# Later weight splits in the first expert, and another order of a word conversion's steps

## The chip, the core and the metric

One NeuronCore of a Trainium2 chip runs the whole program. The metric is the device time of one execution in microseconds. Five engines run side by side, each with its own queue in program order: TensorE (PE in the rows, its weight loads PEld), VectorE (DVE), ScalarE (ACT), GpSimd (POOL) and SyncE (SP, which here only issues DMAs).

## What is computed

Linear attention over 3072 tokens, then a mixture of eight experts where each token goes to one, then a small gated network. Cut to its lines:

```python
state = alpha[t] * state + k[t] v[t]          # per batch and head
y[t]  = q[t] @ state
# mixture: e = argmax(x @ w_gate)
out[e] = gate * sigmoid(x @ w_output_gate) * (relu(x @ w1[e]) @ w2[e])
# gated network; its weights arrive as 64-bit floats
out = ((x @ m1) * (x @ m2) @ m3) @ m_out
```

The gated network's weights are 64-bit floats, and the kernel makes 32-bit floats of them on the chip.

## The kernel before

**Stages.** Attention runs to about 130 us. The experts follow, ordered by size, with room for 464, 440, 424, 408, 396, 388, 376 and 360 tokens; I count them 0 to 7. Between experts 6 and 7 `w_prime` multiplies the last two matrices of the gated network (361 to 394 us). From 419 us on the gated network runs.

**Three-term products.** Each float is split into a high and a low part, and `mm3` (L154 to L157) issues three matmuls: high by high, high by low, low by high. `feed(n)` (L136 to L151) splits n more pieces of weights: ScalarE copies the raw piece to the high part (L146), VectorE subtracts it to get the low part (L147). When both pieces of a raw buffer are split, `load_ahead` has SP load the next raw buffer (L111, or L109 for weights that were converted on the chip). The split pieces live in two rings of four, one for an expert's up half and one for its down half.

**An expert.** The loop at its core has eight up steps (f = 0 to 7) and eight down steps. An up step (`e_up`) is nine matmuls into one of three PSUM banks of `ps_u`, then a ReLU on ScalarE (L822) and on VectorE the low part of it (L823), which frees the bank. A down step (`e_down`) is nine matmuls into three banks that stay. In down steps 1, 3 and 5 `x_split` turns and splits a third of the next expert's tokens (L772 ScalarE, L773 VectorE), and after step 5 GpSimd gathers the tokens of the expert after that (`x_gather`, L754). The order on every engine is the program's order (a manual schedule). So what `feed` puts on ScalarE in a step lies ahead of the ReLU of the next step.

**Steps of a side job.** In each up and down step the loop takes one `next(conv)` (two in expert 0's up half). In expert 0 `conv` is `late_routing`, small VectorE work that finds the tokens' places. From expert 1 on it is `convert_all`: it starts two loads, takes some empty steps, and then converts 23 buffers, each in four steps by `m_convert` (L855) and `words` (L116). A conversion reads pairs of 32-bit words from `mraw` (two buffers): ScalarE takes the absolute value of the high word into `cva` (two buffers, L121) and a scaled copy of the low word into `cvc` (one buffer, L122); VectorE does a maximum (L124), a shift (L125) and a combination with the sign (L127); GpSimd adds the two parts (L130) and writes the result back to memory (L856, `wm_d`). `read()` has SP load the buffer of two conversions later (L852).

Of the kernel before, what the change touches and what calls it, by code (L numbers as in the profile page):

```python
# [11 lines left out]
U32 = mybir.dt.uint32  # L12
ACTF = mybir.ActivationFunctionType
ALU = mybir.AluOpType
# [9 lines left out]
E = 8  # L24
# [28 lines left out]
def attention_then_moe_kernel(ctx, tc, pk0, pka, pkb, wbd_d, wexp, wmlp, cst_d, out):  # L53
    nc = tc.nc
    V, A, G, T, SP = nc.vector, nc.scalar, nc.gpsimd, nc.tensor, nc.sync
# [45 lines left out]
    def load_ahead(after=None):  # L101
        while loaded[0] < min(freed[0] + pools["keep"], len(units)):
            kind, i, parts = units[loaded[0]]
            raw = pools["raw"].tile([128, 2 * NPC], I32, tag="raw", name="raw")
            if after:
                after(raw[:, 0:1], 0)
            if kind == "r":
                for h in range(len(parts)):
                    SP.dma_start(out=raw.bitcast(F32)[:, h * NPC:(h + 1) * NPC], in_=wm_d[i + h])  # L109
            else:  # L110
                SP.dma_start(out=raw.bitcast(F32),  # L111
                             in_=wexp[bass.ds(first[i // 4] + i % 4, 1)].rearrange("o p n -> p (o n)"))
            raws[loaded[0]] = raw
            loaded[0] += 1

    def words(raw, read):  # L116
        w = raw.rearrange("p (n t) -> p n t", t=2)
        lw, hw = w[:, :, 0], w[:, :, 1]
        a, c = [pools["cv"].tile([128, NPC], I32, tag=t, name="cv" + t, bufs=n) for t, n in (("a", 2), ("c", 1))]
        af = a.bitcast(F32)  # L120
        A.activation(out=af, in_=hw.bitcast(F32), func=ACTF.Abs)  # L121
        A.activation(out=c, in_=lw.bitcast(U32), func=ACTF.Copy, scale=2.0 ** -29)  # L122
        yield
        V.tensor_scalar(out=af, in0=af, scalar1=TINY, scalar2=None, op0=ALU.max)  # L124
        V.tensor_scalar(out=a, in0=a, scalar1=3, scalar2=0x3FFFFFF8, op0=ALU.logical_shift_left, op1=ALU.bitwise_and)  # L125
        yield
        V.scalar_tensor_tensor(out=a, in0=hw, scalar=-(1 << 30), in1=a, op0=ALU.bitwise_and, op1=ALU.bitwise_or)  # L127
        read()
        yield
        G.tensor_tensor(out=a, in0=a, in1=c, op=ALU.add)  # L130
        return a.bitcast(F32)


    def ring(key):
        return {"e": key[-1] // 4, "o": 0, "3": 1, "m": key[-1] // 4}[key[0]]

    def feed(n):
        for _ in range(n):
            if fed[0] == len(stream):
                return  # L140
            u, c, key = stream[fed[0]]
            fed[0] += 1
            src = raws[u].bitcast(F32)[:, c * NPC:(c + 1) * NPC]
            tag = "w" + str(ring(key))
            hl = wring.tile([128, 2, NPC], F32R, tag=tag, name=tag)
            A.activation(out=hl[:, 0], in_=src, func=ACTF.Copy)  # L146
            V.tensor_tensor(out=hl[:, 1], in0=src, in1=hl[:, 0], op=ALU.subtract)  # L147
            pieces[key] = hl
            if c == len(units[u][2]) - 1:
                raws.pop(u)  # L150
                freed[0] += 1  # L151
                load_ahead()
# [329 lines left out]
    for j in range(NJ):  # L482
# [22 lines left out]
        if j == 5:  # L505
            A.activation(out=row, in_=cst[:, C_E4:C_E4 + E], func=ACTF.Copy, scale=1024.0)
            V.scalar_tensor_tensor(out=revc, in0=cst[:, C_E4:C_E4 + E], scalar=-1024.0 * E, in1=rev, op0=ALU.mult,
                                   op1=ALU.add)
# [7 lines left out]
        if j in R_RANK:  # L516
# [39 lines left out]
                           op0=ALU.mult, op1=ALU.add)  # L556
# [192 lines left out]
    def x_gather(e, after=None):  # L749
        xg[e] = xg_p.tile([128, 4, DM], F32, tag="xg", name="xg")  # L750
        if after is not None:
            A.activation(out=xg[e][:, :, 0], in_=after, func=ACTF.Copy)
        for i, n in tiles(width(e)):
            G.indirect_dma_start(  # L754
                out=xg[e][0:n, i, :], out_offset=None, in_=x_d[:, :],
                in_offset=bass.IndirectOffsetOnAxis(ap=idx_c[0:n, e, i:i + 1], axis=0))
# [58 lines left out]
    def e_up(e, f, w):  # L815
        m = width(e)
        ps = ps_u.tile([128, CMX], F32, tag="u", name="u")[:, 0:m]
        for k in range(KD):
            sl = slice((f % 2 * KD + k) * 128, (f % 2 * KD + k + 1) * 128)
            mm3(ps, w[:, 0, sl], w[:, 1, sl], xt[e][:, 0, k, 0:m], xt[e][:, 1, k, 0:m], k == 0, k == KD - 1)  # L820
        h = ht_p.tile([128, 2, CMX], F32R, tag=f"h{f}", name=f"h{f}")[:, :, 0:m]
        A.activation(out=h[:, 0, :], in_=ps, func=ACTF.Relu)  # L822
        V.scalar_tensor_tensor(out=h[:, 1, :], in0=ps, scalar=0.0, in1=h[:, 0, :], op0=ALU.max, op1=ALU.subtract)  # L823
        ht[f] = h

    def e_down(e, f, w, ds=range(KD)):
        for d in ds:
            if f == 0:
                dps[d] = ps_d.tile([128, CMX], F32, tag=f"d{d}", name=f"d{d}")[:, 0:width(e)]
            sl = slice(f % 2 * DM + d * 128, f % 2 * DM + d * 128 + 128)  # L830
            mm3(dps[d], w[:, 0, sl], w[:, 1, sl], ht[f][:, 0, :], ht[f][:, 1, :], f == 0, f == KF - 1)

    def e_store(e, col, ds=range(KD)):
        for d in ds:
            A.activation(out=yT[d][:, bass.ds(col, width(e))], in_=dps[d], func=ACTF.Copy)
# [3 lines left out]
    def y_split(g, ds=range(KD)):  # L839
        if ds[0] == 0:  # L840
            ys[g] = ys_p.tile([128, 2, KD, GRP], F32R, tag="ys", name="ys")
        for k in ds:
            src = yT[k][:, g * GRP:(g + 1) * GRP]
            A.activation(out=ys[g][:, 0, k], in_=src, func=ACTF.Copy)
            V.tensor_tensor(out=ys[g][:, 1, k], in0=src, in1=ys[g][:, 0, k], op=ALU.subtract)
# [3 lines left out]
    def m_load(i):  # L849
        if i < N_D:  # L850
            mraw[i] = pools["mr"].tile([128, 2 * NPC], I32, tag="mr", name="mraw")
            SP.dma_start(out=mraw[i], in_=wmlp_w[i])  # L852

    def m_convert(i):
        a = yield from words(mraw.pop(i), lambda: m_load(i + 2))  # L855
        G.dma_start(out=wm_d[i], in_=a)  # L856
        yield
# [94 lines left out]
    def convert_all():  # L952
        m_load(0)
        m_load(1)
        for _ in range(4):
            yield
        for i in range(N_D):
            yield from m_convert(i)

    for e in range(E):  # L960
        if e == 1:
            for _ in conv:
                pass
            lr.close()
            pools["cv"] = cv2.enter_context(tc.tile_pool(name="cvb", bufs=1, reuse_waits="tile"))
            pools["mr"] = cv2.enter_context(tc.tile_pool(name="mr", bufs=2, reuse_waits="tile"))
            conv = convert_all()
        for f in range(KF):
            e_up(e, f, pieces["e", e, f // 2])
            if f % 2:  # L970
                pieces.pop(("e", e, f // 2))
            if e == 0 or f % 2 or e == E - 1:
                feed(1)
            for _ in range(1 if e else 2):
                next(conv, None)
            if e == 0 and f == 1:
                x_gather(1, ht[1][:, 0, 0:4])
        if e == E - 1:
            for d in range(KD):
                for f in range(KF):  # L980
                    e_down(e, f, pieces["e", e, 4 + f // 2], [d])
                e_store(e, offs[e], [d])
                y_split(0, [d])
            for f in range(4):
                pieces.pop(("e", e, 4 + f))
            break
        for f in range(KF):
            e_down(e, f, pieces["e", e, 4 + f // 2])
            if f % 2:
                pieces.pop(("e", e, 4 + f // 2))  # L990
                feed(1)
            next(conv, None)
            if f in (1, 3, 5):
                x_split(e + 1, f // 2, xg[e + 1])
                if f == 5 and e + 2 < E:
                    x_gather(e + 2)
        e_store(e, offs[e])
        if e == E - 2:
            w_prime()
# [136 lines left out]
```

## Time and profile before

| what | us |
|---|---|
| median of 3 runs | 732.04 |
| lowest and highest of them | 731.51, 733.71 |
| the profiled execution, whole | 734.38 |
| its span, first to last instruction | 732.6 |
| TensorE matmul busy | 689.3 (94%) |
| VectorE busy | 400.3 (55%) |
| ScalarE busy | 338.0 (46%) |
| GpSimd busy | 208.4 (28%) |

The profile is of one execution. A row of a timeline gives the start, the duration, the engine, the line and what it writes and reads; in brackets stands how long the engine was idle before it and what ended that. A matmul's end is modelled, so the weight loads (PEld) show more plainly when TensorE really went on.

### The profile page before, as it was taken

To read this page: it belongs to the slowest core of one execution; us is meant where nothing else is said; L and a number is where in the kernel's file an instruction comes from. 1 tells how busy PE (TensorE), PEld (TensorE's weight loads), DVE (VectorE), ACT (ScalarE), POOL (GpSimd) and SP (SyncE) were. 2 spreads that over 40 slices of the span, in tenths; PEclk is the share of its full clock that TensorE was granted. 3 is DMA by queue.
4 is the path that set the end of the run, shared out by engine and by line. 5 is a ranking of instruction groups with operands and counts; after the bars stand their busy time and mean duration, and the time that the engine had idled before them with its cause. 6 is when DMAs were issued, how large, how long until landed. Compare 5 with 4: busy or idle time off the path is not lost.

```text
span 732.6 us, 14570 instructions
## 1 busy us (share of the span) xinstructions
PE 689.3 (94%) x5856; PEld 610.3 (83%) x5856; DVE 400.3 (55%) x723; ACT 338.0 (46%) x666; POOL 208.4 (28%) x233
## 2 busy tenths in 40 slices
PE   6989998789999999998999999999999999999993
PEld 3877787378999998997999988988889889889893
DVE  6989897678689778687734565033132231340320
ACT  3787786344656756656634554133122222331320
POOL 2977685225153544435310000200101101002001
PEclk7999999899999999999999999999999999999997
DMA  8899883464686887878644500100000000001000
GB/s 275 234 256 252 247 261 109 139 214 162 221 296 234 303 285 262 299 250 297 216 150 152 173 1 0 44 1 12 32 1 22 21 1 34 11 1 44 0 12 33
DMA packets 28200, 101.73 MB, mean 139 GB/s; under 512 B 4784, under 2 KB 5208, under 8 KB 28128
## 3 DMA queue, kind: packets, MB, share of 16 engines
q1 hardware_dynamic: 21360, 77.26, 32.9%
q0 software_dynamic: 6624, 23.29, 9.2%
q8 instruction: 47, 0.77, 0.4%
q14 instruction: 25, 0.20, 0.1%
q10 hardware_dynamic: 144, 0.20, 0.1%
HBM read 82.25 MB, written 18.48 MB: 138 GB/s over the span
## 4 chain that ended last, share of the span: by engine, by line
PE 64%; DVE 4%; issue 4%; POOL 3%; ACT 2%; DMA 2%; POOLq 0%; ACTq 0%
PE pab L157 9%; PE pab L155 9%; PE pab L156 9%; PE o L157 4%; PE o L156 4%; PE o L155 4%; PE d L155 4%; PE u L155 4%; PE d L156 4%; PE d L157 4%; PE u L157 4%; PE u L156 4%; POOL cva L130 3%; DVE w L147 2%; ACT w L146 1%
## 5 line engine op out<-in xcount | busy, mean ns | idle before, releaser
L147 DVE TENSOR_TENSOR w<-raw,w 128x768 fp32r<-128x768 f32 x87 | 103.5, 1193 | 57.6 <-ACT w L146 56.3
L1029 DVE TENSOR_TENSOR p_s<-pab,a_s 128x512 f32<-128x512 f32 x48 | 33.2, 692 | 168.4 <-PE pab L157 168.4
L1043 POOL DMA_INDIRECT out_dram<-o_s,idx_o x24 | 23.4, 974 | 331.6 <-ACT o_s L1042 327.9
L155 PE MATMUL pab<-ys,w 128*128 128x512 f32 x288 | 113.8, 395 | 0.0
L157 PE MATMUL pab<-ys,w 128*128 128x512 f32 x288 | 113.8, 395 | 0.0
L156 PE MATMUL pab<-ys,w 128*128 128x512 f32 x288 | 113.8, 395 | 0.0
L146 ACT ACTIVATE w<-raw 128x768 fp32r<-128x768 f32 x87 | 73.0, 842 | 51.6 <-PE d L157 21.2
L1031 ACT ACTIVATE ab<-p_s 128x512 fp32r<-128x512 f32 x48 | 30.4, 634 | 105.5 <-DVE p_s L1029 105.5
L155 PE MATMUL u<-xt,w 128*128 128x464 f32 (+7 forms) x192 | 69.0, 360 | 8.8 <-DVE h L823 8.1
L130 POOL TENSOR_TENSOR cva<-cva,cvc 128x768 int32<-128x768 int32 x23 | 47.0, 2044 | 95.9 <-ACT cva L121 32.4
L156 PE MATMUL u<-xt,w 128*128 128x464 f32 (+7 forms) x192 | 67.6, 352 | 1.5 <-DVE xt L773 1.5
L155 PE MATMUL d<-h,w 128*128 128x464 f32 (+7 forms) x192 | 68.9, 359 | 0.0
L157 PE MATMUL u<-xt,w 128*128 128x464 f32 (+7 forms) x192 | 67.2, 350 | 0.0
L156 PE MATMUL d<-h,w 128*128 128x464 f32 (+7 forms) x192 | 66.9, 348 | 0.0
L157 PE MATMUL d<-h,w 128*128 128x464 f32 (+7 forms) x192 | 66.6, 347 | 0.0
L157 PEld LDWEIGHTS pab<-ys,w 128*128 128x128 f32 x288 | 54.0, 187 | 13.3
L156 PEld LDWEIGHTS pab<-ys,w 128*128 128x128 f32 x288 | 54.0, 187 | 12.9
L155 PEld LDWEIGHTS pab<-ys,w 128*128 128x128 f32 x288 | 54.0, 187 | 12.9
L155 PE MATMUL o<-wpp,ab 128*128 128x384 f32 x192 | 64.2, 334 | 0.0
L157 PE MATMUL o<-wpp,ab 128*128 128x384 f32 x192 | 64.2, 334 | 0.0
L156 PE MATMUL o<-wpp,ab 128*128 128x384 f32 x192 | 64.2, 334 | 0.0
L1032 DVE TENSOR_TENSOR ab<-p_s,ab 128x512 fp32r<-128x512 f32 x48 | 33.2, 693 | 33.6 <-ACT ab L1031 33.6
(187 smaller groups left out, 1436.1 us busy)
## 6 DMA issues: line engine op xcount, KB each, us to landing
raw<-in_wexp_dram SPq DMA_DIRECT2D x32, 768.0 KB, 5.1
mraw<-in_wmlp_dram SPq DMA_DIRECT2D x23, 768.0 KB, 4.3
pb<-in_pkb_dram SPq DMA_DIRECT2D x24, 384.0 KB, 5.0
wm_d<-cva POOLq DMA_DIRECT2D x23, 384.0 KB, 3.9
raw<-wm_d SPq DMA_DIRECT2D x23, 384.0 KB, 3.7
pa<-in_pka_dram SPq DMA_DIRECT2D x42, 192.0 KB, 4.9
x_d<-xs POOLq DMA_DIRECT2D x23, 192.0 KB, 4.6
pa<-in_pka_dram SPq DMA_DIRECT2D x42, 97.5 KB, 5.1
```

The lines of the kernel that those rows point to most:

```text
L130: G.tensor_tensor(out=a, in0=a, in1=c, op=ALU.add)
L146: A.activation(out=hl[:, 0], in_=src, func=ACTF.Copy)
L147: V.tensor_tensor(out=hl[:, 1], in0=src, in1=hl[:, 0], op=ALU.subtract)
L155: T.matmul(out=ps, lhsT=sh, rhs=mh, start=start, stop=False)
L156: T.matmul(out=ps, lhsT=sh, rhs=ml, start=False, stop=False)
L157: T.matmul(out=ps, lhsT=sl, rhs=mh, start=False, stop=stop)
L1029: V.tensor_tensor(out=p_s, in0=pss[1], in1=a_s, op=ALU.mult)
L1031: A.activation(out=t[:, 0], in_=p_s, func=ACTF.Copy)
L1032: V.tensor_tensor(out=t[:, 1], in0=p_s, in1=t[:, 0], op=ALU.subtract)
L1043: G.indirect_dma_start(out=out[:, :], out_offset=bass.IndirectOffsetOnAxis(ap=idx_o[:, n:n + 1], axis=0), in_=o, in_offset=None)
```

## The change

Two places of the loop over experts, one number and the order of `words` are changed.

- In expert 0's up half `feed(1)` is called in steps 3 to 7 and no longer in all eight; in its down half it is called in steps 0 to 5 and 7 and no longer in the odd ones alone. Twelve calls before, twelve after.
- `convert_all` takes five empty steps, not four.
- A conversion's four steps before: both ScalarE passes; maximum and shift; the combination and the load; the addition and the write-back. After: the absolute value; all three VectorE passes; nothing; the copy of the low word, the load, the addition and the write-back.

```diff
         A.activation(out=af, in_=hw.bitcast(F32), func=ACTF.Abs)
-        A.activation(out=c, in_=lw.bitcast(U32), func=ACTF.Copy, scale=2.0 ** -29)
         yield
         V.tensor_scalar(out=af, in0=af, scalar1=TINY, scalar2=None, op0=ALU.max)
         V.tensor_scalar(out=a, in0=a, scalar1=3, scalar2=0x3FFFFFF8, op0=ALU.logical_shift_left, op1=ALU.bitwise_and)
-        yield
         V.scalar_tensor_tensor(out=a, in0=hw, scalar=-(1 << 30), in1=a, op0=ALU.bitwise_and, op1=ALU.bitwise_or)
+        yield
+        yield
+        A.activation(out=c, in_=lw.bitcast(U32), func=ACTF.Copy, scale=2.0 ** -29)
         read()
-        yield
         G.tensor_tensor(out=a, in0=a, in1=c, op=ALU.add)
         return a.bitcast(F32)
...
         m_load(0)
         m_load(1)
-        for _ in range(4):
+        for _ in range(5):
             yield
...
             if f % 2:
                 pieces.pop(("e", e, f // 2))
-            if e == 0 or f % 2 or e == E - 1:
+            if f > 2 if e == 0 else f % 2 or e == E - 1:
                 feed(1)
...
             if f % 2:
                 pieces.pop(("e", e, 4 + f // 2))
+            if f % 2 or e == 0 and f < 6:
                 feed(1)
             next(conv, None)
```

## Rows read from the trace of the kernel before

**Rows 1.** The page, part 2: granted TensorE clock in 40 equal slices, in tenths.
```profile
PEclk7999999899999999999999999999999999999997
```

**Rows 2.** Busy time by stretch (start:end, length, engines with counts, granted clock, DMA).
```profile
154.30:157.70 3.40, 3.40 (x10) 2.93 (x9) 2.87 (x8) 2.75 (x7) 1.82 (x2) 0.50 0.60 193
147.30:181.10 33.80, 31.49 (x161) 26.89 (x160) 28.16 (x70) 14.90 (x26) 14.23 (x14) 0.95 0.56 191
```

**Rows 3.** Waits of weight loads (us, times, longest): 143-181; 200-360, two; 394-420.
```profile
PEld u L155 <- DVE h L823: 2.7, 1, 2.7
...
PEld u L155 <- DVE h L823: 8.6, 11, 1.2
...
PEld u L156 <- DVE xt L773: 1.9, 2, 1.6
...
PEld u L155 <- DVE h L823: 1.4, 2, 0.9
```

**Rows 4.** Timelines of ScalarE and TensorE, expert 0 and the start of expert 1.
```profile
149.99 0.85 ACT L146 ACTIVATE w<-raw 128x768 fp32r<-128x768 f32 x1 [3.42 <-DMA raw<-in_wexp_dram]
...
153.74 0.48 PE L155 MATMUL u<-xt,w 128*128 128x464 f32 x1 [2.31 <-DVE h L823]
...
154.66 0.59 PE L155 MATMUL u<-xt,w 128*128 128x464 f32 x1
155.04 0.59 PE L156 MATMUL u<-xt,w 128*128 128x464 f32 x1
...
157.94 0.37 PE L155 MATMUL u<-xt,w 128*128 128x464 f32 x1
158.15 0.38 PE L156 MATMUL u<-xt,w 128*128 128x464 f32 x1
...
181.73 0.36 PE L155 MATMUL u<-xt,w 128*128 128x440 f32 x1
```

**Rows 5.** Groups by line, 200 to 360 us: busy, mean ns, idle before, releaser.
```profile
L121 ACT ACTIVATE cva<-mraw 128x768 f32<-128x768 f32 x21 | 19.2, 913 | 9.8 <-DMA wm_d<-cva 9.8
L122 ACT ACTIVATE cvc<-mraw 128x768 int32<-128x768 uint32 x21 | 19.1, 909 | 26.5 <-POOL cva L130 26.4
...
L147 DVE TENSOR_TENSOR w<-raw,w 128x768 fp32r<-128x768 f32 x43 | 60.1, 1397 | 21.3 <-ACT w L146 21.0
L127 DVE SCALAR_TENSOR_TENSOR cva<-mraw,cva 128x768 int32<-128x768 int32 x21 | 19.9, 947 | 0.0
L125 DVE TENSOR_SCALAR cva<-cva 128x768 int32<-128x768 int32 x21 | 12.4, 591 | 0.7
L124 DVE TENSOR_SCALAR cva<-cva 128x768 f32<-128x768 f32 x21 | 11.6, 553 | 0.0
...
L130 POOL TENSOR_TENSOR cva<-cva,cvc 128x768 int32<-128x768 int32 x21 | 42.8, 2036 | 75.1 <-ACT cva L121 32.4 <-issue 18.9 <-ACT xt L772 8.8
```

**Rows 6.** Timelines of expert 5's up half: ScalarE, VectorE, GpSimd, weight loads.
```profile
304.68 0.51 ACT L822 ACTIVATE h<-u 128x388 fp32r<-128x388 f32 x1
...
314.00 0.90 ACT L121 ACTIVATE cva<-mraw 128x768 f32<-128x768 f32 x1 [2.30 <-DMA wm_d<-cva]
...
309.42 0.96 DVE L147 TENSOR_TENSOR w<-raw,w 128x768 fp32r<-128x768 f32 x1 [0.17 <-ACT w L146]
...
313.17 2.42 DVE L147 TENSOR_TENSOR w<-raw,w 128x768 fp32r<-128x768 f32 x1
...
307.65 0.62 POOL L856 DMA_DIRECT2D wm_d<-cva  x1 [0.30 <-POOL cva L130]
312.93 1.84 POOL L130 TENSOR_TENSOR cva<-cva,cvc 128x768 int32<-128x768 int32 x1 [4.66 <-issue]
...
309.31 0.19 PEld L155 LDWEIGHTS u<-xt,w 128*128 128x128 f32 x1 [0.25 <-DVE h L823]
311.97 0.19 PEld L155 LDWEIGHTS u<-xt,w 128*128 128x128 f32 x1 [1.13 <-DVE h L823]
```

**Rows 7.** ScalarE's timeline, first up step of expert 7.
```profile
399.03 0.84 ACT L146 ACTIVATE w<-raw 128x768 fp32r<-128x768 f32 x1 [2.15 <-DMA raw<-in_wexp_dram]
```

More of the change, by code (lines that the diff above doesn't have):

```diff
@@ L125, in words @@
         V.tensor_scalar(out=a, in0=a, scalar1=3, scalar2=0x3FFFFFF8, op0=ALU.logical_shift_left, op1=ALU.bitwise_and)
+        V.scalar_tensor_tensor(out=a, in0=hw, scalar=-(1 << 30), in1=a, op0=ALU.bitwise_and, op1=ALU.bitwise_or)
         yield
-        V.scalar_tensor_tensor(out=a, in0=hw, scalar=-(1 << 30), in1=a, op0=ALU.bitwise_and, op1=ALU.bitwise_or)
+        yield
+        A.activation(out=c, in_=lw.bitcast(U32), func=ACTF.Copy, scale=2.0 ** -29)
         read()
-        yield
         G.tensor_tensor(out=a, in0=a, in1=c, op=ALU.add)
```

## The prediction

> **What bounds the kernel now.** I read the page first: TensorE is the bound and runs at the full granted clock nearly everywhere, so only its holes can be won [rows 1]. Then the waits of its weight loads, stretch by stretch, because a hole in the loads is a hole in the matmuls [rows 3]: in the first expert one wait of 2.7 us for the VectorE subtraction at L823 (it frees one of the three `ps_u` banks); from 200 to 360 us, experts 2 to 6 (numbered from 0), eleven such waits, 8.6 us, and two for VectorE's split of the next tokens, 1.9 us; in the last expert 1.4 us. After that the matmul phases have no holes. Both halves of the change aim at those 10.5 and 2.7 us.
>
> *First expert.* ScalarE stood 3.42 us until 149.99 for a raw weight that had not landed: the split that up step 0 puts into its queue [rows 4]. Behind it in the same queue lay the ReLU of step 1; TensorE, which had used up its three banks, waited for VectorE's half of it and started again at 153.74. Then the granted clock fell to half (0.50 from 154.3 to 157.7) [rows 2]: matmuls follow each other every 0.38 us there and every 0.21 us after [rows 4].
>
> *Experts 2 to 6.* Two queues are blocked by the word conversion. On ScalarE, the copy of the low word (L122) waits 26.4 us in 21 conversions for GpSimd's addition, because `cvc` has one buffer and its last reader runs only one step earlier; `Abs` (L121) waits 9.8 us for the write-back of two conversions before [rows 5]. ReLUs lie behind both. On VectorE, the split takes 2.42 us where GpSimd's addition started just before it (312.93 and 313.17), and ends 0.82 us behind that addition's end [rows 6]; the mean over the stretch is 1.40 where a free one takes 0.96 (309.42). Additions that start second are longer in turn, 2.04 in the mean against 1.84 for that one [rows 5, 6].
>
> **Part 1, later splits in the first expert.** Nothing is added or removed. The first split after the start moves from up step 0 to up step 3, those behind it likewise, until down step 5, where both orders stand level; each split's ScalarE copy and VectorE subtraction and the raw load that SP issues behind it move along. The weight of 149.99 is now asked for behind the ReLU of step 3 (about 151.4), when it has long landed. So the 2.7 us [rows 3] go, and with no such hole I expect no half clock: nine matmuls at 0.38 in place of 0.21 are 1.6 us. Sum 4.3. What is late next: VectorE, busy 28.2 of the 33.8 us behind the first ReLU [rows 2], with 4.3 us less to do it in. Its last item that TensorE needs is the third token split of the next expert; that stretch ends with it. Without any idle time it would end at 181.1 - 5.6 = 175.5; I leave 1.8 of idle time in front of raw loads, 177.3. TensorE began expert 1 at 181.73 [rows 4] and needs it six matmuls (1.2) later; 4.3 earlier that is 178.6. It fits by 1.3, so I charge 0.2 only. SP's raw loads of the next expert start up to 2 us later (my estimate from the same queue); a split that has to wait for one then waits in the down half, where no ReLU lies behind it. Value -4.1, bounds -4.4 and -2.1 (room overrun by 2).
>
> **Part 2, the conversion's order.** Work stays the same: two ScalarE passes (0.91 each), three VectorE passes (0.55, 0.59, 0.95), one addition (1.84 when free), one load on SP, one write-back on GpSimd's queue [rows 5, 6]. With the fifth empty step at the start, `Abs` falls on up and down steps 1 and 5, the three VectorE passes on 2 and 6, nothing on 3 and 7, the copy, the load and the addition on 4 and 0. Step by step:
>
> - The copy of L122 now follows the previous addition by four steps, over 6 us: its 26.4 us of waiting [rows 5] go. New wait: the addition now waits for this copy. Behind it on GpSimd lie only the write-back and, once per expert, the token gather, needed an expert later.
> - VectorE: before, `max`, shift and a split stood ahead of the ReLU half of step 2; now the three passes stand on steps without a split. The additions start at steps 0 and 4, behind the copy, where VectorE has only PSUM reads or nothing to do, except as below.
> - SP: the load of the word pairs leaves one to two steps later and behind the raw load of steps 3 and 7; the write-back likewise goes out later. `Abs` is one step later too, so room shrinks by a step. I measured one write-back from 307.65 to the `Abs` at 314.00 that it held, 6.3 us [rows 6]. In the new order up step 5 may still wait a microsecond for it, but behind step 5 no ReLU holds a bank that this expert's up half still needs. So I cost it nothing; if that cover fails it is part of the bounds.
>
> A walk through expert 5, the second narrowest of these: its first ReLU is at 304.68 [rows 6] in both orders. The copy behind it ends near 305.97, the addition runs from 306.1 to 307.94, the split of step 1 ends 0.82 later, 308.76; then ReLU half of step 2, three passes (0.55, 0.59, 0.95) and ReLU half of step 3, done near 311.6. Before, the same half of step 2 came so late that TensorE stood 1.13 us until 311.97, with a hole of 0.25 at 309.31 ahead of it [rows 6]. In the new order, step 2's half is done at 309.2 and TensorE asks for it at 310.3 (311.97 - 1.13 less that hole and the 0.3 that the shorter of the two token-split waits cost [rows 3]); step 3's is late by 0.0 to 0.1. So 10.5 us of holes less 0.3 for such edges.
>
> The narrow place: the split of step 3 starts near 311.5; the addition of step 4 starts behind ReLU 4 and the copy, near 312.1. Half a microsecond decides who is first; in expert 6, with shorter matmuls, about 0.25. If the addition is first, the split ends 0.82 behind it, some 2 us late, and the ReLU half of step 4 holds up step 7 by about 1.9. The Trainium skill's page SBUF — State Buffer, section "Who interferes with whom", says the same as a rule: the port pair that VectorE and GpSimd share goes to whoever starts first, for its whole instruction. The trace agrees, with 2.42 us for the split behind an addition and a mean of 2.04 for the additions [rows 5, 6]; by that rule the order of starts alone makes the sum 9.0 or 4.8. I take 1.2 off for it (the narrowest expert, a bit more than even). Value -9.0, bounds -10.5 (all holes) and -4.8 (collisions in experts 4 to 6, three times 1.9 kept).
>
> **Part 3, the spill into the last expert.** Four empty steps and 23 conversions of four made 96 steps, exactly experts 1 to 6. With five, the last copy (0.91), addition (1.84) and write-back fall into up step 0 of expert 7, where a split stands on every step. That split waits for its weight until 399.03 [rows 7]; the copy comes behind it and holds the next ReLU, which TensorE waited for (1.4 us in all, two holes [rows 3]). Then the addition blocks a split, 1.46 us by 2.42 against 0.96 [rows 6]. ScalarE's next wait for a weight swallows part. Value +0.7, bounds 0 and +1.4. The vacated steps in front of `w_prime` free nothing, TensorE has no hole there.
>
> **Sum.** -4.1 -9.0 +0.7 = -12.4. Against the profiled execution's own time, 734.38: 722.0. The median of the three runs, 732.04, is 2.34 lower: 719.6.
>
> **Rivals.**
> 1. *The collision moves to step 4.* The addition beats the split in experts 4 to 6. For it: margins of 0.25 to 0.5 us in a hand-made queue. Against: GpSimd's start follows three ScalarE instructions. 5.7 us stay: 734.38 -4.1 -4.8 +0.7, as a median 723.8.
> 2. *The conversion's waits only change their names.* The write-back or the pair load, asked for later, hold `Abs` at steps where ReLUs count. For it: 6.3 us for a write-back. Against: two whole conversions lie between. Only the first expert pays: -4.1 +0.7, 728.6.
> 3. *The first expert doesn't pay.* VectorE is the bound of its down half and hands the hole back: -9.0 +0.7, 723.7.
> 4. *Slower.* The collision at step 4 comes in all of experts 2 to 6 and its 1.9 us stop is long enough for the clock to halve, as after the 2.7 us stop [rows 2, 3]; stops of up to 1.6 us were not followed by that [rows 1, 3]. Then 1.9 + 1.6 = 3.5 in five experts is 17.5 for the 10.5 taken away: +7.0 -4.1 +0.7 = +3.6, 735.6. It decides once step 4's copy starts 0.8 us earlier against VectorE than I reckon, and only if 1.9 us of rest suffice.
>
> **How the numbers follow.** Forecast 0.68; rival 1 0.17; rival 2 0.06; rival 3 0.05; rival 4 0.04. The lowest sum is -4.4 -10.5 +0 = -14.9, 717.1, with run-to-run spread 716.5; the highest within the forecast and rivals 1 and 3 is -2.1 -4.8 +1.4 = -5.5, 726.5, say 727. That leaves rivals 2 and 4 and a little of the edges outside. A measurement of this kernel tells 0.3%, 2.2 us, from no change. All but rival 4 lie beyond it on the fast side, rival 2 by little, so some of it goes to "same": faster 0.92, same 0.04, slower 0.04.
>
> **What would show it.** Part 1: no ScalarE wait for a raw weight ahead of the second ReLU, no hole near 151, clock 1.00 through 160, and expert 1 starting about 4 us earlier. Part 2: L122 with no wait for GpSimd; L121's wait for the write-back much below 9.8 or only at steps 5; the split's mean between 1.0 and 1.2, with at most one blocked split per expert in its up half, behind step 0's addition; the eleven holes down to a handful of a tenth. Rival 1 would show as one hole of nearly 2 us ahead of up step 7. Part 3: a copy and an addition near the start of expert 7 and a slightly larger hole there. I am wrong if a wait for DMA takes ScalarE's time in up steps 0 to 4, or if the token split of the next expert becomes the late item.

## The result and the profile after

The changed kernel takes 726.65 us in the median of five runs (725.14 to 727.38), beside 732.04 (731.01 to 734.06) before: a ratio of 0.9912, interval 0.9891 to 0.9932. I had forecast 719.6 with a range of 716.5 to 727.0. So it is faster and within the range, but by 5.4 us where I had worked out 12.4, at the far end.

The page of the kernel after: its first lines, part 2's granted clock, and two lines of part 6 (size, median us from issue to landing).

```profile
PE 687.8 (95%) x5856; PEld 612.2 (84%) x5856; DVE 397.1 (55%) x723; ACT 338.9 (47%) x666; POOL 209.2 (29%) x233
...
PEclk9999999799999999998999999999999999999998
...
mraw<-in_wmlp_dram SPq DMA_DIRECT2D x23, 768.0 KB, 6.7
wm_d<-cva POOLq DMA_DIRECT2D x23, 384.0 KB, 5.6
```

Against [rows 1] the slice around 136 us reads 7 where it read 8, and there is a new 8 around 335 us. On the page of before the last two medians are 4.3 and 3.9 us: the same bytes now land later.

The waits of the weight loads after, for the stretches of [rows 3]: 200 to 352 us, then 384 to 412 (L155, L156). Between 143 and 181 us there is no row for `h` any more, only `issue` of 0.7 us in all.

```profile
PEld u L155 <- DVE h L823: 3.4, 2, 2.4
...
PEld u L155 <- DVE h L823: 2.0, 2, 1.2
PEld d L156 <- DVE h L823: 0.3, 1, 0.3
```

Of eleven holes two are left, 3.4 us, both behind 320 us, in expert 6. Groups by line after, 200 to 352 us, to be read against [rows 5]:

```profile
L128 ACT ACTIVATE cvc<-mraw 128x768 int32<-128x768 uint32 x21 | 19.1, 911 | 0.0
L121 ACT ACTIVATE cva<-mraw 128x768 f32<-128x768 f32 x21 | 19.0, 903 | 10.0 <-DMA wm_d<-cva 7.1 <-DMA mraw<-in_wmlp_dram 2.9
L147 DVE TENSOR_TENSOR w<-raw,w 128x768 fp32r<-128x768 f32 x42 | 52.2, 1249 | 18.0 <-ACT w L146 17.2
```

The copy's 26.4 us of waiting are gone. The split's mean fell from 1397 to 1249 ns. But `Abs` waits as long as before, 10.0 us, now for a load too.

To place the difference I took the length of each half of an expert (from its first weight load to the first of the next half). Columns are kernels, a number behind a name being another profiled execution of it; halves that are not listed are equal within 0.15 us in all.

```
              before before_2 after after_2 after_3 p1_feeds p2_words drain c_early  a3   a3_drain a3_drain_2 b_c2 b_small
start of e0   143.07 141.50  140.99 142.47 140.44  143.09   141.26  141.49 140.93 142.81  141.19   142.46  142.44 138.87
e0 up          19.75  19.38   17.02  17.06  15.61   17.38    19.33   16.92  17.09  15.61   18.05    18.14   19.38  19.47
e0 down        18.71  18.70   18.71  18.71  18.70   18.70    18.71   18.71  18.73  18.71   18.70    18.71   19.16  18.99
e2 up          14.12  14.12   13.88  13.88  13.88   14.11    13.88   13.88  13.88  13.88   13.88    13.88   14.12  13.88
e3 up          14.44  14.48   13.41  13.41  13.41   14.49    13.41   13.41  14.04  13.41   13.41    13.41   13.98  13.41
e4 up          14.88  14.89   12.96  12.96  12.96   15.22    12.96   12.96  13.74  12.96   12.96    12.96   13.83  12.96
e5 up          15.23  15.25   12.81  12.81  12.81   15.39    12.81   12.81  13.62  12.81   12.81    12.81   13.76  12.81
e6 up          16.49  16.44   18.16  14.80  16.46   17.41    15.82   14.86  15.58  14.13   12.52    12.37   14.86  13.72
e7 up          13.16  13.09   13.80  13.52  13.65   13.44    13.83   12.79  12.89  13.72   13.29    12.89   13.09   12.84
e7 down        11.92  11.91   12.18  11.96  11.99   11.90    12.01   11.85  11.97  11.98   11.85    11.91   11.91   11.92
```

The two profiled executions are 7.7 us apart: 2.1 because expert 0 starts earlier, 2.7 in expert 0, 5.6 in experts 2 to 5, less 1.8 lost in expert 6 (0.1 of it in its down half) and 0.9 in expert 7. The 2.1 are not the change's: nothing before expert 0 was touched, and the starts of one and the same kernel lie 1.6 to 2.0 us apart (143.07 and 141.50 before; 140.99, 142.47 and 140.44 after).

**Expert 5 came out as walked through.** Timelines of its up half after (start, duration, engine, line; in brackets the idle time before), to be read against [rows 6]:

```profile
296.66 0.51 ACT L822 ACTIVATE h<-u 128x388 fp32r<-128x388 f32 x1
297.03 0.93 ACT L128 ACTIVATE cvc<-mraw 128x768 int32<-128x768 uint32 x1
...
305.85 0.92 ACT L121 ACTIVATE cva<-mraw 128x768 f32<-128x768 f32 x1 [0.26 <-DMA wm_d<-cva]
...
299.23 1.49 DVE L147 TENSOR_TENSOR w<-raw,w 128x768 fp32r<-128x768 f32 x1 [0.17 <-ACT w L146]
303.63 0.95 DVE L147 TENSOR_TENSOR w<-raw,w 128x768 fp32r<-128x768 f32 x1
...
305.63 1.49 DVE L147 TENSOR_TENSOR w<-raw,w 128x768 fp32r<-128x768 f32 x1
...
298.05 1.86 POOL L130 TENSOR_TENSOR cva<-cva,cvc 128x768 int32<-128x768 int32 x1 [1.66 <-ACT cvc L128]
304.16 2.15 POOL L130 TENSOR_TENSOR cva<-cva,cvc 128x768 int32<-128x768 int32 x1 [3.34 <-ACT cvc L128]
```

The split of step 1 ends at 300.72, 0.81 us behind the addition's end at 299.91. The split of step 3 starts 0.53 us ahead of the second addition and takes 0.95 us; the addition pays instead, with 2.15. I had reckoned with half a microsecond. The split of step 5 then starts while that addition still runs (until 306.31), and takes 1.49 us: two splits of this half are blocked, and neither makes a hole.

**Expert 6 didn't.** Timelines after: ScalarE, weight loads, GpSimd, VectorE and SP.

```profile
314.06 0.90 ACT L121 ACTIVATE cva<-mraw 128x768 f32<-128x768 f32 x1 [2.44 <-DMA wm_d<-cva]
...
329.21 0.89 ACT L121 ACTIVATE cva<-mraw 128x768 f32<-128x768 f32 x1 [3.57 <-DMA wm_d<-cva]
329.99 0.85 ACT L822 ACTIVATE h<-u 128x376 fp32r<-128x376 f32 x2
...
331.11 0.19 PEld L155 LDWEIGHTS u<-xt,w 128*128 128x128 f32 x1 [2.40 <-DVE h L823]
...
333.62 0.29 PEld L155 LDWEIGHTS u<-xt,w 128*128 128x128 f32 x1 [1.01 <-DVE h L823]
...
318.11 2.44 POOL L130 TENSOR_TENSOR cva<-cva,cvc 128x768 int32<-128x768 int32 x1 [5.47 <-DVE cva L125]
320.84 0.56 POOL L856 DMA_DIRECT2D wm_d<-cva  x1 [0.30 <-POOL cva L130]
...
333.25 1.81 POOL L130 TENSOR_TENSOR cva<-cva,cvc 128x768 int32<-128x768 int32 x1 [4.67 <-DVE cva L125]
...
333.48 2.40 DVE L147 TENSOR_TENSOR w<-raw,w 128x768 fp32r<-128x768 f32 x1
...
318.86 0.81 SPq L109 DMA_DIRECT2D raw<-wm_d  x2
319.78 0.36 SPq L852 DMA_DIRECT2D mraw<-in_wmlp_dram  x1
```

`Abs` of up step 1 stands in ScalarE's queue until the write-back of 320.84 has landed, 3.57 us; two ReLUs lie right behind it (329.99, x2), and TensorE stops for 2.40 us and once more for 1.01. Behind that, the addition of step 4 starts 0.23 us ahead of the split of step 3, which takes 2.40 us: the narrow place of rival 1, lost here too. The loads of SP left 1.1 to 2.0 us ahead of the write-back of 320.84. And that write-back left late itself: the `Abs` of down step 1 had stood 2.44 us until 314.06 for the write-back of 306.60, so VectorE's three passes came late, and the addition behind them at 318.11. The busy times of the two flights, expert 5's write-back (issued at 300.20) and this one (columns as in [rows 2]: the last three are clock, DMA share and GB/s), and of the stretch behind the hole:

```profile
300.20:305.83 5.63, 5.63 (x34) 5.63 (x33) 5.46 (x10) 3.93 (x7) 2.29 (x2) 1.00 0.79 279
320.84:329.18 8.34, 8.18 (x48) 7.87 (x46) 7.60 (x9) 4.45 (x9) 6.51 (x6) 1.00 0.96 321
...
332.60:339.30 6.70, 6.19 (x20) 5.60 (x20) 6.63 (x10) 2.79 (x5) 2.40 (x2) 0.50 0.55 189
```

The same 384 KB take 8.34 us instead of 5.63. The clock then was at 0.50, its lower level of 1.2 GHz, from 332.6 to 339.3.

The DMA share alone (0.96 against 0.79) doesn't tell long flights from short ones. Three other write-backs, two of the kernel after and one of the kernel before:

```profile
306.60:314.04 7.44, 7.44 (x45) 7.40 (x44) 6.74 (x8) 3.42 (x6) 2.98 (x3) 1.00 0.79 281
312.08:315.23 3.15, 3.15 (x21) 3.11 (x20) 1.40 (x2) 1.17 (x3) 0.56 (x1) 1.00 0.67 209
...
315.07:318.20 3.13, 2.43 (x14) 2.10 (x14) 2.89 (x5) 2.34 (x5) 0.59 (x1) 1.00 0.99 357
```

One takes 7.44 us at a share of 0.79, another 3.13 at 0.99. What goes with the flight is which loads SP issued just ahead (timelines after, GpSimd and SP):

```profile
306.60 0.59 POOL L856 DMA_DIRECT2D wm_d<-cva  x1 [0.30 <-POOL cva L130]
...
312.08 0.56 POOL L856 DMA_DIRECT2D wm_d<-cva  x1 [0.30 <-POOL cva L130]
...
304.61 0.33 SPq L111 DMA_DIRECT2D raw<-in_wexp_dram  x1
305.05 0.37 SPq L852 DMA_DIRECT2D mraw<-in_wmlp_dram  x1
312.64 0.33 SPq L111 DMA_DIRECT2D raw<-in_wexp_dram  x1
```

The first of these two left behind a raw load and a pair load, the second 0.56 us ahead of them. In the trace of after, the sixteen write-backs that left 1.1 to 2.2 us behind a pair load and a raw load landed 4.8 to 8.3 us after their issue, and the five that left 0.6 us ahead of a raw load 3.1 to 3.3 us after it. In the kernel before, thirteen of the first twenty-one had only the pair load ahead of them and took 3.0 to 4.8 us; the eight with a raw load ahead too took 5.3 to 6.6.

### The profile page after: what moved, and what is told of

Same layout as the page of the kernel before. It is cut to its first block, busy times and chain, and to the rows that moved or that the text cites. A ratio compares the mean times of both kernels' runs of the same rounds, so it can differ in the third digit from the quotient of the medians.

```text
span 724.9 us, 14568 instructions
## 1 busy us (share of the span) xinstructions
PE 687.8 (95%) x5856; PEld 612.2 (84%) x5856; DVE 397.1 (55%) x723; ACT 338.9 (47%) x666; POOL 209.2 (29%) x233
## 4 chain that ended last, share of the span: by engine, by line
PE 69%; DMA 6%; DVE 2%; issue 1%; ACT 1%; POOL 0%; POOLq 0%; SPq 0%; ACTq 0%
PE pab L155 9%; PE pab L156 9%; PE pab L157 9%; PE u L156 5%; PE u L155 5%; PE u L157 5%; PE o L155 4%; PE o L156 4%; PE o L157 4%; PE d L155 4%; PE d L156 4%; PE d L157 4%; DMA wm_d<-cva 4%; DMA mraw<-in_wmlp_dram 1%; PE x L759 1%
## 5 line engine op out<-in xcount | busy, mean ns | idle before, releaser
L147 DVE TENSOR_TENSOR w<-raw,w 128x768 fp32r<-128x768 f32 x87 | 95.8, 1105 | 53.4 <-ACT w L146 51.6
L155 PE MATMUL pab<-ys,w 128*128 128x512 f32 x288 | 113.8, 395 | 0.0
L156 PE MATMUL pab<-ys,w 128*128 128x512 f32 x288 | 113.8, 395 | 0.0
L130 POOL TENSOR_TENSOR cva<-cva,cvc 128x768 int32<-128x768 int32 x23 | 44.9, 1953 | 126.2 <-ACT cvc L128 94.6
L155 PE MATMUL u<-xt,w 128*128 128x464 f32 (+7 forms) x192 | 68.9, 359 | 4.6 <-DVE h L823 4.0
L155 PE MATMUL d<-h,w 128*128 128x464 f32 (+7 forms) x192 | 68.9, 359 | 0.0
L156 PE MATMUL u<-xt,w 128*128 128x464 f32 (+7 forms) x192 | 68.6, 357 | 0.2 <-DVE xt L773 0.2
L157 PE MATMUL u<-xt,w 128*128 128x464 f32 (+7 forms) x192 | 68.4, 356 | 0.0
L156 PE MATMUL d<-h,w 128*128 128x464 f32 (+7 forms) x192 | 67.0, 349 | 0.0
L156 PEld LDWEIGHTS pab<-ys,w 128*128 128x128 f32 x288 | 54.0, 187 | 13.0
L155 PEld LDWEIGHTS pab<-ys,w 128*128 128x128 f32 x288 | 54.0, 187 | 12.9
L155 PE MATMUL o<-wpp,ab 128*128 128x384 f32 x192 | 64.2, 334 | 0.0
L156 PE MATMUL o<-wpp,ab 128*128 128x384 f32 x192 | 64.2, 334 | 0.0
```

What stands on the lines that cost most here:

```text
L155: T.matmul(out=ps, lhsT=sh, rhs=mh, start=start, stop=False)
L156: T.matmul(out=ps, lhsT=sh, rhs=ml, start=False, stop=False)
L157: T.matmul(out=ps, lhsT=sl, rhs=mh, start=False, stop=stop)
```

## The experiments

My theory after the result: each part does what it was made for, part 1 for its hole alone, and the rest was lost in expert 6 to the write-back and in expert 7 to the spill. The rivals: the collision on VectorE's port, the clock, and one part that spoils the other.

**The feeds alone (p1_feeds)**, on the kernel before:

```diff
-            if e == 0 or f % 2 or e == E - 1:
+            if f > 2 if e == 0 else f % 2 or e == E - 1:
                 feed(1)
...
+            if f % 2 or e == 0 and f < 6:
                 feed(1)
```

> The later splits alone (the change in the two feed conditions); conversion as before. Theory A (the hole of 2.7 us in expert 0 goes, but a stretch at half clock stays somewhere near the start of the experts): expert 0's up half 17.0 us against 19.75 before, everything from expert 1 on as before, total 2.7 us below before, about 729.3. Theory B (the half clock that the changed kernel showed at 141 us belongs to that one execution): up half 15.3 to 15.5, total 4.3 below, 727.7.

Measured: 731.61 us (727.3 to 733.8), ratio 0.9967 (0.9948 to 0.9987). Expert 0's up half is 17.38 us, against 19.75 and 19.38 before; all other halves stay or get up to 0.9 longer (expert 6, by longer waits for its tokens, 2.5 us in place of 1.6; why is not shown), so the medians differ by 1.2 us on this chip (732.81 before), not by 2.7. No weight load of expert 0 waits for `h`, and yet there is half the clock, in another place. Its busy times in that half:

```profile
143.10:160.40 17.30, 17.30 (x71) 14.98 (x72) 14.59 (x33) 10.55 (x19) 3.80 (x4) 0.87 0.50 164
```

TensorE is busy for all of the 17.30 us, and the mean clock is 0.87: a half-clock stretch from 140.8 to 147.7 reaches into it. So the hole goes with this part, the half clock doesn't: theory A.

**The conversion's order alone (p2_words)**: the diff of `words` and the fifth empty step, without the two conditions of the feeds.

> The conversion's new order with five empty steps alone; the splits of expert 0 as before. If the parts add up: up halves of experts 2 to 5 shorter by 0.2, 1.0, 1.9 and 2.4 as in the changed kernel, expert 6 and 7 longer, together 2.7 below before, about 729.3, and expert 0 as before with 19.75 in its up half. Rival (expert 6's long stop in the changed kernel is an accident of that execution): expert 6's up half 13 to 14 us in place of 18.2, total 7 below before, 725.

Measured: 727.13 us (726.52 to 728.24), ratio 0.9917 (0.9889 to 0.9945). Experts 2 to 5 are as in the whole change to 0.01 us, expert 0 as before (19.33). Expert 6's up half, 15.82 us, lies between the two expectations. The parts don't spoil each other, and most of the gain is this one's: 5.7 us (732.81 to 727.13).

**The spill taken out (drain)**: what is left of the conversion is issued ahead of `w_prime`.

```diff
         if e == E - 2:
+            for _ in conv:
+                pass
             w_prime()
```

> The changed kernel, but the last conversion is finished ahead of w_prime, so that no copy, addition or write-back falls into expert 7. Theory: expert 7's up half 13.2 in place of 13.8 and its down half 11.9 in place of 12.2, so 0.9 us below the changed kernel, 725.8. Rival (expert 7's larger hole comes from its weights' landing): both halves as in the changed kernel.

Measured: 723.61 us (719.83 to 725.21), ratio 0.9864 (0.9815 to 0.9914). Expert 7 shrinks to 12.79 and 11.85 us, 1.0 and 0.3 less than after. The rest of what the medians show is expert 6 (14.86 us), which this edit doesn't touch. Expert 7's waits were 2.0 and 0.3 us; what remains:

```profile
PEld u L155 <- DVE h L823: 1.0, 2, 0.9
```

**The copy and the load one step earlier (c_early)**: this takes from the addition its releaser, the copy just ahead of it, so that it may start before the split of step 3.

```diff
         yield
-        yield
         A.activation(out=c, in_=lw.bitcast(U32), func=ACTF.Copy, scale=2.0 ** -29)
         read()
+        yield
         G.tensor_tensor(out=a, in0=a, in1=c, op=ALU.add)
```

> The changed kernel, but the copy of the low word and the load of the next pairs stand one step earlier, on the steps 3 and 7 that were empty; the addition can start when that copy is done. Theory of the narrow place (who starts first, VectorE's split of step 3 or GpSimd's addition): the addition now starts 0.7 us earlier and beats the split, one hole of about 1 us ahead of up step 7 in each of experts 3 to 5, their up halves 0.8 to 1.2 us longer than in the changed kernel. Theory of expert 6 (Abs held by a write-back that leaves late and flies long): its write-backs and pair loads leave about 1.5 us earlier, so the stop of 2.4 us shrinks to 1.2 or less, no half clock, up half 14 to 15.5 in place of 18.2. Sum about 726. Rival (no narrow place, holes stay away): 722 to 723.

Measured: 726.38 us (725.12 to 727.63), ratio 0.9912 (0.9877 to 0.9946). Experts 3, 4 and 5 lose 0.63, 0.78 and 0.81 us. Expert 5's timeline, then the waits of the weight loads from 235 to 312 us:

```profile
304.72 1.84 POOL L130 TENSOR_TENSOR cva<-cva,cvc 128x768 int32<-128x768 int32 x1 [4.03 <-ACT cvc L127]
304.84 2.53 DVE L147 TENSOR_TENSOR w<-raw,w 128x768 fp32r<-128x768 f32 x1
...
307.90 0.19 PEld L155 LDWEIGHTS u<-xt,w 128*128 128x128 f32 x1 [0.87 <-DVE h L823]
...
PEld u L155 <- DVE h L823: 2.4, 3, 0.9
```

The addition wins by 0.12 us and the split takes 2.53 us in place of 0.95: the narrow place of my first rival, where I had put it. The Trainium skill's page SBUF — State Buffer, section "Who interferes with whom", has it that the one that issues first keeps the shared ports for its whole instruction; the trace agrees, with 0.12 us of lead for the addition here and 0.53 for the split in the kernel after. The hole that follows is 0.7 to 0.9 us, not the 1.9 that I had priced it at. Expert 6 takes 15.58 us, just over the expectation: its `Abs` of step 1 still waits 2.21 us, the stop ahead of step 5 is 1.05 us, and there is no half clock.

**A third buffer for `cva` (a3)**: every third conversion works in columns of a constant tile that only attention reads. With it no `Abs` waits for a write-back.

```diff
+        n_cv[0] += 1
+        if n_cv[0] % 3:
+            a = pools["cv"].tile([128, NPC], I32, tag="a", name="cva", bufs=2)
+        else:
+            a = cst[:, C_CAUSAL:C_CAUSAL + NPC].bitcast(I32)
```

> The changed kernel with a third buffer for the absolute values (it lies in constants that are no longer used), so that Abs waits for the write-back of three conversions before. Theory (expert 6's stop comes from the write-back): no wait of Abs for a write-back, the stop in expert 6 falls below 1 us, half 13.5 to 15 in place of 18.2; Abs may wait up to 1 us for its pair load instead. Total 723 to 724. Rival (the pair load is as late): the stop stays above 1.5 us, Abs waits for the load of its pairs, half 15 or more.

Measured: 721.39 us (717.9 to 722.66), ratio 0.9843 (0.9801 to 0.9884). Groups by line from 200 to 352 us, and expert 6's timeline (GpSimd, VectorE, weight loads):

```profile
L126 ACT ACTIVATE cva<-mraw 128x768 f32<-128x768 f32 x14 | 12.7, 905 | 2.7 <-DMA mraw<-in_wmlp_dram 2.7
L126 ACT ACTIVATE cst<-mraw 128x768 f32<-128x768 f32 x7 | 6.3, 907 | 1.8 <-DMA mraw<-in_wmlp_dram 1.8
...
330.85 1.83 POOL L135 TENSOR_TENSOR cva<-cva,cvc 128x768 int32<-128x768 int32 x1 [3.12 <-ACT cvc L133]
330.92 2.58 DVE L152 TENSOR_TENSOR w<-raw,w 128x768 fp32r<-128x768 f32 x1
334.01 0.19 PEld L160 LDWEIGHTS u<-xt,w 128*128 128x128 f32 x1 [1.46 <-DVE h L828]
```

The wait for `wm_d` is gone, and expert 6 takes 14.13 us. `Abs` of step 1 now waits 0.58 us for its pairs. What holds the half is the narrow place: the addition was first by 0.07 us, and the hole ahead of step 7 is 1.46 us. Expert 0's up half here is 15.61 us, with the clock at 1.00 throughout and the same instructions as in the kernel after.

**Both mends (a3_drain, a3_drain_2)**: the diffs of drain and a3 together, on two chips.

> The third buffer and the last conversion finished ahead of w_prime, both. If the two add up: expert 6's up half 13.5 to 15, expert 7's halves 12.8 and 11.9, total 721.5 to 722.5, below both kernels. Rival (the gain of the drained kernel was of its expert 6 by chance): as the third buffer alone less 1.0 at most.

> Third buffer and drained conversion again: 719 to 720.5, 5 below the changed kernel on the same chip; expert 6's up half 12.5 if VectorE's split starts ahead of GpSimd's addition in step 4, 13.9 to 14.1 if the addition is first by a tenth of a microsecond.

Measured: 719.36 us (716.36 to 721.31), ratio 0.9817 (0.9780 to 0.9854), and on another chip 720.79 us (717.49 to 722.91), ratio 0.9820 (0.9794 to 0.9845). Expert 6 takes 12.52 and 12.37 us; expert 7's up half is 13.29 and 12.89, where I had expected 12.8. In the first of them its split came ahead of the addition by 0.12 us (VectorE, then GpSimd):

```profile
331.54 0.95 DVE L152 TENSOR_TENSOR w<-raw,w 128x768 fp32r<-128x768 f32 x1
331.66 2.55 POOL L135 TENSOR_TENSOR cva<-cva,cvc 128x768 int32<-128x768 int32 x1 [3.11 <-ACT cvc L133]
```

This version beats both kernels, the one after by 0.5% (724.17 to 720.79) on the chip where both were timed; I had expected 5 us there, and it is 3.4.

**Both kernels again (before_2, after_2, after_3)**, without an edit.

> The kernel before once more, unchanged, for a second profile of expert 0. Theory A (a stretch at half clock comes near the start of the experts in every execution, and the one at 154 us was not the price of the 2.7 us hole): half clock may lie at 138 to 147 us this time, and then expert 0's up half is 19.3 to 19.8 with a hole of only 2 us in sum. Theory B (the hole calls the half clock): half clock directly behind the hole at 151 again, none between 138 and 147.

> The changed kernel once more, unchanged. If expert 6's stop of 2.4 us and the half clock behind it are how this kernel runs: up half of expert 6 near 18.2 again. If the write-back's flight varies from execution to execution: a stop between 1 and 2.5 us, and the half clock only with the longest of them; up half 14.5 to 16 without it. All other halves as in the first profile within 0.3 us.

> The changed kernel, unchanged, timed beside the next one on one chip: 724 to 727; expert 6's up half between 14.8 and 18.2, all others as in its first two profiles.

Measured: 732.40 and 724.22 us, of one execution each, and 724.17 us for after_3 (722.56 to 724.83), ratio 0.9879 (0.9864 to 0.9894). The kernel before, in its second execution: the waits of its weight loads from 141 to 181 us, then busy times of two stretches.

```profile
PEld u L155 <- DVE h L823: 3.1, 3, 1.7
...
141.20:144.60 3.40, 3.10 (x7) 2.43 (x8) 3.12 (x5) 3.34 (x6) 0.00 (x0) 0.50 0.00 2
154.00:158.00 4.00, 3.35 (x15) 2.37 (x14) 3.63 (x7) 3.08 (x6) 3.35 (x3) 1.00 0.82 270
```

It has the holes, 3.1 us in three pieces, and the clock behind them is 1.00. Its half-clock stretch comes at 141.2, ahead of the holes. Three other kernels with the old order of splits (p2_words, b_c2, b_small) have 2.0 to 3.0 us of such holes, and no half clock behind them either.

**Which wait made which hole in experts 3 to 5 (b_c2, b_small)**, both on the kernel before. The first gives `cvc` a second buffer, so that its copy waits for no addition; the second lets the addition work on 32 of its 768 columns, so that it holds VectorE's port for only 0.24 us (the low words of the other columns are left out).

```diff
+        if n_cv[0] % 2:
+            c = pools["cv"].tile([128, NPC], I32, tag="c", name="cvc", bufs=1)
+        else:
+            c = cst[:, C_CAUSAL:C_CAUSAL + NPC].bitcast(I32)
```

```diff
-        G.tensor_tensor(out=a, in0=a, in1=c, op=ALU.add)
+        G.tensor_tensor(out=a[:, 0:32], in0=a[:, 0:32], in1=c[:, 0:32], op=ALU.add)
```

> The kernel before with a second buffer for the scaled low words (in constants that are no longer used), so that their copy does not wait for GpSimd's addition; the order of steps as before. Theory (of the two holes in each up half of experts 4 to 6, the first, ahead of step 5, comes from ScalarE's wait for the addition, the second, ahead of step 7, from VectorE's split behind GpSimd's addition): the first hole goes or falls below 0.3, the second stays near 1.0; up halves of experts 4 and 5 about 13.9 and 14.2 in place of 14.9 and 15.2. Rival (VectorE's own order, three passes and a split ahead of the ReLU half, makes the first hole): both holes stay, halves as before.

> The kernel before with GpSimd's addition cut to 32 of 768 columns; the low words of the other columns are left out of the weights. It takes about 0.1 us in place of 1.84, so neither ScalarE's copy waits for it nor does VectorE's split collide with it. Theory: both holes go, up halves of experts 4 and 5 near 13.0 and 12.9, as in the changed kernel, all splits below 1.0 us. The difference to the kernel with the second low-word buffer is the price of the collision, about 1.0 in each. Rival (the order of VectorE's passes alone makes a hole): a hole of 0.5 to 1.1 ahead of step 5 stays.

Measured, one execution each: 729.16 and 721.76 us. Waits and groups of b_c2 from 240 to 315 us, then a group of b_small in the same stretch (it has no wait for `h` there at all); before has `PEld u L155 <- DVE h L823` with 5.6 us in seven holes in the same experts (240 to 318 us).

```profile
PEld u L160 <- DVE h L828: 2.5, 3, 1.0
L152 DVE TENSOR_TENSOR w<-raw,w 128x768 fp32r<-128x768 f32 x21 | 34.7, 1658 | 6.6 <-ACT w L151 6.4
...
L147 DVE TENSOR_TENSOR w<-raw,w 128x768 fp32r<-128x768 f32 x22 | 21.0, 957 | 14.2 <-ACT w L146 14.0
```

Without the copy's wait the holes ahead of up step 5 are gone, those ahead of step 7 stay (0.64, 0.88, 1.01 in experts 3 to 5), and the split's mean is 1658 ns. With a short addition, which ends both the copy's wait and the blocking, it is 957 ns, there is no hole, and experts 3 to 5 are as short as after. So about half of those holes were the copy's, half the port's, and the new order takes both. In expert 6, which the first expectation takes in, a hole of 1.2 us ahead of step 5 stays (1.16 and 1.17); what makes it there isn't shown.

## Why the prediction was right and wrong

**Part 1: the hole right, the clock wrong.** In no kernel with the later splits does a weight load of expert 0 wait for `h`, and ScalarE's copies no longer wait for raw weights in its up half. They wait in the down half instead (2.51 and 4.87 us in after), where no ReLU lies behind them, as I had reckoned. VectorE's room held: the down half is 18.70 to 18.73 us in all of them, so rival 3 falls. But the term was 4.1 us, and between executions with 3.1 to 3.4 us of half clock in that half it measures 2.3 to 2.7 (from 19.38 and 19.75 to 17.02 and 17.06). The step that failed is the 1.6 us that I put down to the hole from [rows 2, 4]. In before_2 no half clock follows 3.1 us of holes; in the kernel after, p1_feeds and after_2 there is half clock in that half without such a hole. Where none fell into it (after_3, a3) the half is 15.61 us, which is the 4.1 below the first profile: the number of the forecast, by where the clock fell and not by the hole. What decides where it falls between 138 and 158 us stays open: after had 3.4 us of it from 141.4, after_3 none in expert 0, and in both TensorE had stood 1.44 us just ahead of expert 0's first transposes (until 139.10 and 138.52).

**Part 2, experts 2 to 5: right.** I had every hole gone there but small edges, and they are, in all eight executions with the new order and no other copy step: 0.24 + 1.03 + 1.92 + 2.42 = 5.6 us. The copy's 26.4 us went, and the split's mean is 1.25 where I had named 1.0 to 1.2. Two splits of each up half are blocked, behind step 0's addition, as foreseen, and behind step 4's, which I had not foreseen (in expert 5 both take 1.49); neither costs a hole.

**Part 2, expert 6: wrong, and most of the miss.** The step was "if that cover fails": I costed the later write-back at nothing since I looked at up step 5 alone, behind which no ReLU counts. The `Abs` that it held was that of step 1, with all ReLUs behind it: the wait for DMA in up steps 0 to 4 that I had named as a sign of being wrong. The `Abs` of steps 1 and 5 both stand five steps behind the addition whose write-back they wait for, as before the change, but steps aren't time: ScalarE gets to step 1's in expert 6 at 325.6 (329.21 less 3.57), 4.8 us after the issue at 320.84, and to step 5's in expert 5 at 305.6, 5.4 us after its issue at 300.20. The one flight that I had read, 6.3 us in [rows 6], was longer than either. And SP's pair load, moved behind the raw loads, puts four transfers within 2.0 us. Over the executions the length of the half goes with that one wait (times in us; at -0.12 the split was first):

```
                               after  after_3 p2_words c_early after_2 drain   a3   a3_drain
Abs of step 1 waits for wm_d    3.57    3.09     2.44    2.21    1.42   1.18  none    none
hole ahead of step 5            2.40    1.92     1.28    1.05    0.26   0.16  none    none
addition of step 4 first by     0.23    0.23     0.23    0.23    0.23   0.23  0.07   -0.12
e6 up                          18.16   16.46    15.82   15.58   14.80  14.86 14.13   12.52
```

That is rival 2's mechanism, in one expert of the five that I gave it. The hole ahead of step 5 grows with the wait; two more come with any wait of 1.2 us or more. One of 1.0 us lies ahead of step 6, for the ReLU half of step 3 then stands behind VectorE's three passes. One of 1.3 us lies ahead of step 7 (not in after, which was at half the clock by then), for the late passes let the addition of step 4 start ahead of the split of step 3: rival 1's collision, in all six of these executions, and in a3 by 0.07 us without that wait. So expert 6 had two narrow places, and where the first made `Abs` wait, it decided the second. The longest also has the half clock; after_3 has holes of 4.2 us in all at a clock of 1.00. Against before, expert 6 lost 1.7, stood even and gained 1.7 us in the three executions of the kernel after, where I had counted on a gain of about 3 of the 9.0.

That the loads issued just ahead lengthen the write-back's flight is read from the rows; no run moved those loads alone. The Trainium skill's page DMA: Bandwidth & Descriptors, section "Issuing engines are not separate DMA queues", says that transfers of all issuing engines interleave on the same 16 engines, and the trace agrees: a write-back from GpSimd's queue takes 8.34 us behind SP's loads and 3.15 just ahead of them. Which of the loads costs it most stays open.

**Part 3: right.** I had +0.7 (0 to 1.4). Expert 7 grew by 0.4 to 0.9 us in three executions of the kernel after, and drain gives it back (its two halves are 0.4 us shorter than before).

**The sum**, then: instead of -4.1 -9.0 +0.7, about -2.3 to -2.7 in expert 0 with the half clock in it both times, -5.6 in experts 2 to 5, 0 give or take 1.7 in expert 6 and +0.6 in expert 7: -7.3 with the smaller of the first, and between -9.0 and -5.6 by what expert 6 does. The medians differ by 5.4 on one chip, and by 8.9 on the chip of after_3 (733.07 to 724.17). That 5.4 lies within my range is luck: its end at 727.0 was added up from collisions in three experts and an overrun in expert 0, while the failed cover was called a part of the bounds without a price. The sum with both mends, -2.3 -5.6 -4.0 -0.1 = -12.0, is near what I had forecast for the change, and the measured 11.8 and 12.3 us (731.18 to 719.36, 733.07 to 720.79) are near it; the two profiled executions had a longer half clock in expert 0, which is only 1.2 to 1.7 us shorter in them.

## What to carry to other kernels

When a step is moved, check every consumer of the transfers that it issues at each of its steps, and in microseconds, not in steps: steps that only queue up behind one another give no time. A transfer's duration read from before holds only while the same transfers are issued ahead of it, so where loads are moved together, price the wait with the longer flight, or give it another buffer. A late start is passed on: one write-back that lands late delays the conversion that needs its buffer, and with that the write-back of that conversion. And don't charge a half-clock stretch to the hole in front of it from one execution: take a second one of the same kernel first.

## What the runs showed of the hardware

- The place of a half-clock stretch changes between executions of the same program: behind expert 0's first steps (154.3) and ahead of them (141.2) in the kernel before; at 141.4, at 143.0 and not at all in expert 0 in the kernel after. One of 3.4 us costs about 1.45 us there (17.06 against 15.61).
- Of holes in TensorE's work near 2 us, one of 2.40 was followed by half the clock (after, 332.6 to 339.3), one of 1.92 (after_3, expert 6) and one of 2.12 (p1_feeds, expert 6) were not.
- A split that starts behind an addition ends 0.81 to 0.82 us behind that addition's end, though it started 1.18, 0.12 and 0.07 us behind its start: 0.81 in expert 5 after, 0.81 in c_early, 0.82 in a3. On margins this small the recorded starts don't settle who waits: a split that starts 0.05 us ahead of an addition in expert 6 after (325.78, 2.73 us) and one 0.12 us ahead in expert 4 of b_c2 (272.75, 2.81 us) also end 0.83 behind it, while the one 0.12 us ahead in a3_drain takes 0.95.
- The 384 KB write-back took 3.13 us at a DMA share of 0.99 (before, 315.07), 5.63 and 7.44 at 0.79 and 8.34 at 0.96 (after): in the trace of after, 4.8 to 8.3 us behind a raw load and a pair load, 3.1 to 3.3 us ahead of them.
